# Idle matmuls at the start, a reordered opening, fold copies on ScalarE and Strassen's scheme in half of one second layer

## Chip, core and metric

The kernel runs on one core of one Trainium2 chip. A core has five engines with a queue each: TensorE (PE, matrix products, with its weight loads shown apart as PEld), VectorE (DVE), ScalarE (ACT), GpSimd (POOL) and SyncE (SP, which here issues nearly all DMAs). The metric is device time in microseconds. Five runs of the kernel before gave a median of 847.75 us (846.78 to 854.08).

## The reference

Sparse attention over four batches, eight heads, 768 tokens of 64 channels, followed by a Fourier mixing block with a two-layer network. Everything is float32.

```python
# attention: a band of 2*16-1 neighbours, and 24 block summaries
k_sum = k.reshape(B, H, nb, block, D).max(axis=3)      # block = 32, nb = 24
v_sum = v.reshape(B, H, nb, block, D).mean(axis=3)
scores_l = where(|i - j| < 16, scale * q @ k.T, -1e9)
scores_s = scale * q @ k_sum.T + log(block)
a = softmax(concat(scores_l, scores_s)) ;  out = a @ concat(v, v_sum)
# mixing: x is (4, 768, 512)
mixed = real(fft(fft(x, axis=1), axis=2))
u = x + mixed
un = (u - mean(u)) / sqrt(var(u) + 1e-6)
ch = maximum(un @ w_ch1, 0) @ w_ch2                    # 512 -> 2048 -> 512
return u + ch
```

The two weight matrices arrive as float64 and are turned into float32 on the chip, piece by piece, with bit operations (convert, `words` tiles).

## The kernel before

The program works batch by batch: attention (`gen_attention`), Fourier mixing and normalisation (`gen_fourier`), hidden layer (`gen_hidden`) and output layer (`gen_out`). These are generators; `drive` interleaves their steps, so that attention of the next batch and the Fourier part of the next batch are recorded between the matrix products of the present one. A scheduler then fixes one order for each engine[...]. A `high_priority` of 600 lets attention and Fourier steps move ahead.

**Attention.** A pair of heads (g = 0 to 3, a step of the loop in `gen_attention`) is: load keys and queries, turn them with matmuls (`prepare`, L668 for batch 0, L676 for others, copies on ScalarE L670/L678, block maxima on VectorE L679), scores (L695 and L699 in batch 0, L735 and L751 later), exponentials on ScalarE (L701, L741), a mask product on VectorE (L560), then values (L718, L767). Line L560 is the helper `tt`, so it stands for nearly all VectorE tensor products; groups are told apart by tile names. The values' block sums are made from raw loads (`block_sums`, tiles `vb`, `vbs`): on GpSimd (L563) for most batches, on VectorE for batch 1, whose sums are made early. In batch 0 `sum_values` multiplies them with a selector (L709) and ScalarE copies the result into the values' tile (L710, 1.43 us); this stands ahead of `prepare` for the next pair.

**Fourier part.** The batch's x is folded on VectorE: sums and differences of its halves (tiles `sd`, `zw`, `fg`, all views of `fold`), with three small copies a half (L990, L994, L997). TensorE makes y (L1014 and L1018) from `fold` and a table `fs`, ScalarE copies y (L1020, L1021), TensorE makes mx (L1038, L1040 in batch 0; L963, L965 later), VectorE adds it to x and takes statistics, un is transposed (unt, L1079) into u. In batch 0, `keep_busy` gives TensorE four 128x512 products without use (L952) while the fold runs.

**Hidden layer.** Eight steps j, each by Strassen's seven products on half blocks (L1101, three PSUM tiles X, Y, Z, combined by ScalarE copies L1111, L1116, L1118 and VectorE additions; relus on ScalarE in batch 0 L1108, on VectorE later L1106). Strassen's scheme as used: four sums of left blocks (`_left_sums`, S1 to S4), four of right blocks (`_right_sums`, T1 to T4), seven products, additions.

**Output layer.** `gen_out(b, c)` handles half c of the hidden units. In batches 1 to 3 it uses Strassen's scheme (L1167): left sums of h on VectorE (tiles `s`), right blocks of w2 with their sums in tiles `w2`, 84 products of 128x256. In batch 0 it is a plain product for both c (L1142): 48 products of 128x512, because w2's right sums do not exist yet; they are made in batch 1 (`get_w2`), which loads four blocks, forms three more and writes six back to DRAM for batches 2 and 3.

**Weights.** `gen_weights` follows a hand-written `plan` of pieces, each not before a named stage; `make` converts two halves, adds left sums for w1, and stores the result in DRAM (`dw1`, `dw2`). It runs beside the first batch.

Four PSUM banks serve attention (`abank`), four the rest (`bank`). Tiles with a tag and `bufs=n` share n buffers; a new tile waits for the last reader of the old one.

Of the kernel before, what the change touches and what calls it, by code (L numbers as in the profile page):

```python
# [9 lines left out]
FP = mybir.dt.float32  # L10
# [6 lines left out]
P = 128  # L17
# [469 lines left out]
def _main_program(ctx, tc, q, k, v, moe_w_ch1, moe_w_ch2, out):  # L487


    nc = tc.nc  # L490
    B, H, S, D = q.shape
    DM = H * D
# [91 lines left out]
    def block_sums(b, gg):  # L584

        f = BLOCK // 4
        n = f * D
        if done_weights:
            raw = room(f"vb_{b}_{gg}")
            raw = [raw[0:4 * nb, n * i:n * (i + 1)] for i in range(4)]  # L590
        else:

            raw = [bpool.tile([P, NC, P], FP, tag="s", bufs=5, name=f"vb_{b}_{gg}_{i}").rearrange("p n t -> p (n t)")
                   [0:4 * nb] for i in range(4)]
        for i in range(4):
            fetch(out=raw[i], in_=v[b, 4 * gg:4 * gg + 4].rearrange("h (n f) d -> (h n) (f d)", f=BLOCK)
                  [:, n * i:n * (i + 1)])
        vb = spool.tile([4 * nb, D], FP, tag="vbs", bufs=2, name=f"vbs_{b}_{gg}")

        add = tt if b == 1 else gtt  # L600
        add(raw[0], raw[0], raw[1], ADD)
        add(raw[2], raw[2], raw[3], ADD)
        add(raw[0], raw[0], raw[2], ADD)
        if b == 1:
            nc.vector.tensor_reduce(out=vb, in_=raw[0].rearrange("p (f d) -> p d f", d=D), op=ADD, axis=AX.X)
# [12 lines left out]
        return vw_bufs[g % 2].rearrange("p (e n) d -> p e n d", e=2)  # L618

    def load_values(b, g):  # L620
        if g % 2 and following(b, g, 1):
            block_sums(*divmod((b * NP + g + 1) // 2, NP // 2))
        (load_wide_values if is_wide(b) else load_narrow_values)(b, g)

# [159 lines left out]
    def following(b, g, n):  # L784
        i = b * NP + g + n
        return divmod(i, NP) if i < B * NP else None

    def gen_attention(b):
        x = bpool.tile([P, NST, DM], FP, tag="x", bufs=2, name=f"x_{b}")
        x_of[b] = x  # L790
        for g in range(NP):
            p = (wide_scores if is_wide(b) else scores)(b, g)
            yield
            if is_wide(b):
                sum_values(b, g)
            else:
                sum_scores(b, g, p[1])
            n1, n2 = following(b, g, 1), following(b, g, 2)
            early = (b, g) == (0, NP - 1)
            if early:  # L800
                wide_values(b, g, p, x)
            if n1:
                with tc.issue_after(marks["last av"]) if early else ExitStack():
                    prepare(*n1)

            for n in {(0, 1): (), (0, 2): (2,), (0, 3): (2, 3)}.get((b, g), (3,)):
                n = following(b, g, n)
                if n:
                    load(*n)
            yield  # L810
            if not early:
                if is_wide(b):
                    wide_values(b, g, p, x)
                else:
                    values(b, g, *p, x)
            if n2:
                load_values(*n2)
            if (b, g) == (0, 0):
                load_raw(2)
            yield  # L820


# [47 lines left out]
    def make(f, j):  # L870


        if f == 1:
            w = bpool.tile([P, 7, 2, P], FP, tag="w1", bufs=3, name=f"w1_0_{j}")
            wv, to = w.rearrange("p a k n -> p a (k n)"), dw1[j].rearrange("p a k n -> p a (k n)")
        else:
            w = wv = bpool.tile([P, 7, HD], FP, tag="w2", bufs=NC, name=f"w2_0_{j}")
            to = dw2[j]
        for hh in range(2):
            yield from convert((f, j, hh), wv[:, 2 * hh:2 * hh + 2].rearrange("p a n -> p (a n)"))  # L880
        if f == 1:
            _left_sums(tt, lambda i: wv[:, i])
        else:

            to, wv = to[:, 0:4], wv[:, 0:4]
# [29 lines left out]
    def get_w2(b, j):  # L915
        w = bpool.tile([P, 7, HD], FP, tag="w2", bufs=NC, name=f"w2_{b}_{j}")
        if b == 0:
            return
        wt[2, b, j] = w
        if b == 1:  # L920
            fetch(out=w[:, 0:4], in_=dw2[j][:, 0:4])
            _right_sums(tt, lambda i: w[:, i])
            fetch(out=dw2[j][:, 1:7], in_=w[:, 1:7])
        else:
            fetch(out=w, in_=dw2[j])
# [46 lines left out]
    def gen_fourier(b):  # L972
# [10 lines left out]
        for par in range(2):  # L983
            sd, zw, fg = fold[:, 0], fold[:, 1], fold[:, 2 - 2 * par]
            tt(sd, x[:, 0:HT, :], x[:, HT:NST, :], SUB if par else ADD)
            keep_busy(b, par, sd)
            tt(zw[:, :, 0:HD], sd[:, :, 0:HD], sd[:, :, HD:DM], ADD)
            tt(zw[:, :, HD:DM], sd[:, :, 0:HD], sd[:, :, HD:DM], SUB)
            keep_busy(b, par, zw)
            nc.vector.tensor_copy(out=zq[:, par], in_=zw[:, :, Q])  # L990
            nc.vector.memset(fg[:, :, Q:Q + 1], 0.0)
            tt(fg[:, :, 1:Q], zw[:, :, 1:Q], zw[:, :, HD - 1:Q:-1], ADD)
            tt(fg[:, :, Q + 1:HD], zw[:, :, 1:Q], zw[:, :, HD - 1:Q:-1], SUB)
            nc.vector.tensor_copy(out=fg[:, :, 0:DM:HD], in_=zw[:, :, 0:DM:HD])  # L994
            tt(fg[:, :, HD + 1:HD + Q], zw[:, :, HD + 1:HD + Q], zw[:, :, DM - 1:HD + Q:-1], SUB)
            tt(fg[:, :, HD + Q:DM - 1], zw[:, :, HD + 1:HD + Q], zw[:, :, DM - 1:HD + Q:-1], ADD)
            ins = nc.vector.tensor_copy(out=fg[:, :, DM - 1:DM], in_=zw[:, :, HD + Q:HD + Q + 1])  # L997
            fgs.append(fg)
            yield
        marks["fold", b] = ins.ins  # L1000
# [132 lines left out]
    def gen_out(b, c):  # L1133
        x, h = x_of[b], wt["h", b]
        js = range(NC * c, NC * (c + 1))
        if b == 0:

            for t in range(NST):
                ps = bank([P, DM], f"o_{b}_{c}_{t}")
# [4 lines left out]
                    if n % 2 == 0:  # L1144
                        yield
                tt(x[:, t, :], ps, x[:, t, :], ADD)
                if NC * (c + 1) == NJ:
                    fetch(out=out[b, P * t:P * (t + 1), :], in_=x[:, t, :])
            issued.add(("o", b, c))
            return  # L1150
        for i in range(HT):
# [42 lines left out]

    nc.scalar.dma_start(out=ident, in_=dr["ident"].ap())
    load(0, 0)
    fetch(out=wide, in_=dr["wide"].ap())
    nc.scalar.dma_start(out=count, in_=dr["count"].ap())
    nc.scalar.dma_start(out=sel, in_=dr["sel"].ap())
# [119 lines left out]
```

## Time and profile before

| what | us |
|---|---|
| median of five runs | 847.75 |
| the profiled execution | 847.71 |
| its span on the core | 845.9 |
| TensorE busy / idle in the span | 812.5 / 33.4 |
| output layer of batch 0 on TensorE (L1142, 192 records) | 84.9 |
| longest waits of TensorE: hx for ScalarE's copy of h (5 times) | 6.0 |
| qk for the DMA of keys (2 times) | 5.7 |
| the busy products for the fold (once) | 5.3 |
| value sums for GpSimd's block sums (once) | 3.3 |

How to read it: a float32 product appears as two records in the trace, so 48 products are 96 records. A wait is put down to what came last. Idle time of engines other than TensorE costs nothing by itself.

### The profile page before, as it was taken

The numbers are of one execution on the slowest core, as the hardware profiler recorded it, in microseconds if no ns is written. First come the engines' busy times: TensorE is split into PE (matmuls) and PEld (weight loads), VectorE is DVE, ScalarE is ACT, GpSimd is POOL, SyncE is SP. The second block draws the span as 40 slices with busy tenths as digits, with TensorE's granted clock in tenths as the row PEclk, the third lists the DMA queues.
The fourth block names the chain that finished last, engine by engine and source line by source line (L and its number), as shares of the span: only waits on it lengthen the run. The fifth ranks groups of instructions, "written<-read, shape, count | busy, mean of one in ns | idle before, by whom it ended". The sixth has DMA issues, their size and how long they took to land.

```text
span 845.9 us, 14497 instructions
## 1 busy us (share of the span) xinstructions
PE 812.5 (96%) x6006; PEld 568.5 (67%) x6006; DVE 480.4 (57%) x1115; ACT 230.1 (27%) x473; POOL 38.3 (5%) x44
## 2 busy tenths in 40 slices
PE   5979998999999999999999999999999999999997
PEld 4847755545556555787667875688667885786586
DVE  2487996986976543544357943443337953532352
ACT  3524666552721113122232104120321012101100
POOL 3200012003000200001000000000000000000000
PEclk8989999999999999999999999999999999999999
DMA  9997595979523274454843236403411326205001
GB/s 215 227 281 164 146 243 180 267 247 300 194 79 131 75 273 136 115 112 160 237 107 98 72 131 218 113 24 83 166 60 55 113 63 248 88 1 217 1 27 53
DMA packets 102858, 120.94 MB, mean 143 GB/s; under 512 B 50592, under 2 KB 83584, under 8 KB 102784
## 3 DMA queue, kind: packets, MB, share of 16 engines
q1 hardware_dynamic: 102240, 119.77, 48.7%
q8 instruction: 49, 0.80, 0.4%
q10 hardware_dynamic: 544, 0.17, 0.1%
q14 instruction: 25, 0.20, 0.1%
HBM read 95.80 MB, written 24.12 MB: 142 GB/s over the span
## 4 chain that ended last, share of the span: by engine, by line
PE 80%; DVE 10%; ACT 6%; DMA 2%; issue 1%; ACTq 0%; SPq 0%; DVEq 0%
PE hx L1101 18%; PE ox L1167 13%; PE o L1142 9%; PE hz L1101 9%; PE oz L1167 7%; PE hy L1101 4%; PE y L1014 4%; PE oy L1167 3%; DVE x L560 3%; PE sc L735 2%; PE mx L963 1%; ACT qt L678 1%; ACT kt L678 1%; PE unt L1079 1%; PE sc L695 1%
## 5 line engine op out<-in xcount | busy, mean ns | idle before, releaser
L1101 PE MATMUL hx<-u,w 128*128 128x384 f32 x512 | 186.1, 492 | 8.0 <-ACT h L1111 6.0
L1101 PEld LDWEIGHTS hx<-u,w 128*128 128x128 f32 x512 | 94.6, 190 | 74.5 <-ACT h L1111 9.3
L1101 PE MATMUL hz<-u,w 128*128 128x384 f32 x256 | 93.2, 486 | 0.0
L1142 PE MATMUL o<-w,h 128*128 128x512 f32 x192 | 84.9, 595 | 0.0
L1101 PEld LDWEIGHTS hz<-u,w 128*128 128x128 f32 x256 | 48.7, 190 | 33.9 <-ACT h L1118 0.2
L1167 PE MATMUL ox<-w,s 128*128 128x256 f32 x288 | 69.0, 381 | 0.4 <-DVE x L560 0.3
L1167 PE MATMUL oz<-w,s 128*128 128x256 f32 x288 | 68.7, 379 | 0.0
L1167 PE MATMUL ox<-w,h 128*128 128x256 f32 x288 | 67.0, 380 | 0.0
L1142 PEld LDWEIGHTS o<-w,h 128*128 128x128 f32 x192 | 35.7, 190 | 41.8 <-issue 39.7
L560 DVE TENSOR_TENSOR x<-ox,x 128x256 f32<-128x256 f32 x72 | 30.2, 422 | 55.7 <-PE ox L1167 55.7
L1167 PEld LDWEIGHTS ox<-w,h 128*128 128x128 f32 x288 | 54.5, 190 | 8.3
L1167 PEld LDWEIGHTS ox<-w,s 128*128 128x128 f32 x288 | 54.0, 190 | 8.4 <-DVE x L560 1.2
L1167 PEld LDWEIGHTS oz<-w,s 128*128 128x128 f32 x288 | 54.5, 190 | 7.2
L560 DVE TENSOR_TENSOR h<-hx,h 128x384 f32<-128x384 f32 x32 | 17.8, 556 | 71.2 <-PE hx L1101 71.2
L560 DVE TENSOR_TENSOR h<-hy,h 128x384 f32<-128x384 f32 x32 | 17.8, 556 | 57.2 <-PE hy L1101 54.0
L1111 ACT COPY h<-hx 128x384 f32<-128x384 f32 x32 | 15.3, 477 | 121.6 <-PE hx L1101 109.9
L1101 PE MATMUL hy<-u,w 128*128 128x384 f32 x128 | 46.5, 486 | 0.0
L679 DVE TENSOR_REDUCE km<-kt 128x24 f32<-128x768 f32 x16 | 15.2, 952 | 39.0 <-ACT kt L678 25.1
L1127 ACT ACTIVATE h<-hx 128x384 f32<-128x384 f32 x32 | 15.7, 490 | 79.1 <-PE hx L1101 79.1
L1014 PE MATMUL y<-fs,fold 128*128 128x193 f32 x192 | 37.1, 336 | 0.0
L1014 PEld LDWEIGHTS y<-fs,fold 128*128 128x128 f32 x192 | 31.3, 190 | 7.8 <-issue 6.1
L1101 PEld LDWEIGHTS hy<-u,w 128*128 128x128 f32 x128 | 24.4, 190 | 16.9
(125 smaller groups left out, 1103.6 us busy)
## 6 DMA issues: line engine op xcount, KB each, us to landing
w<-dw SPq DMA_DIRECT2D x40, 896.0 KB, 5.6
words<-in_moe_w_ch_dram SPq DMA_DIRECT2D x32, 512.0 KB, 6.5
vw<-in_v_dram SPq DMA_DIRECT2D x47, 192.0 KB, 5.6
dw<-w SPq DMA_DIRECT2D x8, 896.0 KB, 7.5
kn<-in_k_dram SPq DMA_DIRECT2D x16, 384.0 KB, 4.8
qn<-in_q_dram SPq DMA_DIRECT2D x16, 384.0 KB, 5.5
vb<-in_v_dram SPq DMA_DIRECT2D x32, 192.0 KB, 5.2
out_dram<-x SPq DMA_DIRECT2D x24, 256.0 KB, 2.5
```

Source lines behind the costliest of these rows:

```text
L560: nc.vector.tensor_tensor(out=out, in0=in0, in1=in1, op=op)
L678: nc.scalar.copy(out=dst[D * e:D * (e + 1), s:S:2], in_=ps[D * s:D * (s + 1)])
L679: nc.vector.tensor_reduce(out=km[:, 0:nb], in_=kt[:, W:W + S].rearrange("p (n f) -> p n f", f=BLOCK), op=ALU.max, axis=AX.X)
L695: nc.tensor.matmul(ps[e][0:WK, n - n0, :], kt[rows, QB * n:QB * n + WK], qt[rows, QB * n:QB * (n + 1)], start=True, stop=True)
L735: nc.tensor.matmul(ps[h][r:r + 64, i, :], kt[rows, o:o + 64], qt[rows, o:o + BLOCK], start=True, stop=True)
L963: nc.tensor.matmul(out, y[:, g], table, start=True, stop=last, skip_group_check=True)
L1014: nc.tensor.matmul(y, fgs[par][:, st, P * g:P * (g + 1)], fs[par][:, g % 2, st, :], start=(st == 0), stop=(st == HT - 1))
L1101: nc.tensor.matmul(ps, w[:, a, kk, :], u[:, r, kk, :], start=start and kk == 0, stop=stop and kk == 1, skip_group_check=True)
L1111: nc.scalar.copy(out=c11, in_=X)
L1127: nc.scalar.activation(out=c21, in_=X, func=AF.Relu)
L1142: nc.tensor.matmul(ps, h[:, n, hf, P * t:P * (t + 1)], wt[2, b, j][:, 2 * hf:2 * hf + 2, :], start=(n, hf) == (0, 0), stop=(n, hf) == (NC ...
L1167: nc.tensor.matmul(ps, left[a][:, n, :], wt[2, b, j][:, r, :], start=start and n == 0, stop=stop and n == NC - 1, skip_group_check=True)
```

## The change

Six edits:

- Two products of a zeroed tile are put at the very start on TensorE; the tile is zeroed by GpSimd.
- In the first head pair of batch 0, `sum_values` comes after `prepare` of the next pair, and the first weight loads come ahead of the value loads for g = 2.
- Block sums for batch 1: the first half goes to GpSimd; the second stays on VectorE and moves from the attention of batch 1 to the end of the Fourier part of batch 0.
- Left sums of the first w1 piece wait until the fold of batch 0 is done.
- The three small copies of the fold go from VectorE to ScalarE.
- `gen_out(0, 1)` uses Strassen's scheme. So `make` forms the right sums of w2 for j = 4 to 7 and stores all seven blocks, and batch 1 loads these seven instead of forming and writing them.

```diff
@@ block_sums
-        add = tt if b == 1 else gtt
+        add = tt if (b, gg) == (1, 1) else gtt
...
-        if b == 1:
+        if (b, gg) == (1, 1):
             nc.vector.tensor_reduce(out=vb, in_=raw[0].rearrange("p (f d) -> p d f", d=D), op=ADD, axis=AX.X)
@@ load_values
-        if g % 2 and following(b, g, 1):
+        if g % 2 and following(b, g, 1) and (b, g) != (1, 1):
             block_sums(*divmod((b * NP + g + 1) // 2, NP // 2))
@@ gen_attention
-            if is_wide(b):
+            if not is_wide(b):
+                sum_scores(b, g, p[1])
+            elif g:
                 sum_values(b, g)
-            else:
-                sum_scores(b, g, p[1])
...
                 with tc.issue_after(marks["last av"]) if early else ExitStack():
                     prepare(*n1)
+            if (b, g) == (0, 0):
+                sum_values(b, g)
...
+            if (b, g) == (0, 0):
+                load_raw(2)
             if n2:
                 load_values(*n2)
-            if (b, g) == (0, 0):
-                load_raw(2)
@@ make
-        if f == 1:
+        if (f, j) == (1, 0):
+            while ("fold", 0) not in issued:
+                yield
+            with tc.issue_after(marks["fold", 0]):
+                _left_sums(tt, lambda i: wv[:, i])
+        elif f == 1:
             _left_sums(tt, lambda i: wv[:, i])
-        else:
+        elif j < NC:
             to, wv = to[:, 0:4], wv[:, 0:4]
+        else:
+            _right_sums(tt, lambda i: wv[:, i])
@@ get_w2
-        if b == 1:
+        if b == 1 and j < NC:
             fetch(out=w[:, 0:4], in_=dw2[j][:, 0:4])
             _right_sums(tt, lambda i: w[:, i])
             fetch(out=dw2[j][:, 1:7], in_=w[:, 1:7])
@@ gen_fourier
-            nc.vector.tensor_copy(out=zq[:, par], in_=zw[:, :, Q])
+            nc.scalar.copy(out=zq[:, par], in_=zw[:, :, Q])
...
-            nc.vector.tensor_copy(out=fg[:, :, 0:DM:HD], in_=zw[:, :, 0:DM:HD])
+            nc.scalar.copy(out=fg[:, :, 0:DM:HD], in_=zw[:, :, 0:DM:HD])
...
-            tt(fg[:, :, HD + Q:DM - 1], zw[:, :, HD + 1:HD + Q], zw[:, :, DM - 1:HD + Q:-1], ADD)
-            ins = nc.vector.tensor_copy(out=fg[:, :, DM - 1:DM], in_=zw[:, :, HD + Q:HD + Q + 1])
+            nc.scalar.copy(out=fg[:, :, DM - 1:DM], in_=zw[:, :, HD + Q:HD + Q + 1])
+            ins = nc.vector.tensor_tensor(out=fg[:, :, HD + Q:DM - 1], in0=zw[:, :, HD + 1:HD + Q],
+                                          in1=zw[:, :, DM - 1:HD + Q:-1], op=ADD)
@@ gen_out
-        if b == 0:
+        if (b, c) == (0, 0):
...
-                if NC * (c + 1) == NJ:
-                    fetch(out=out[b, P * t:P * (t + 1), :], in_=x[:, t, :])
@@ the start of the program
     load(0, 0)
+    zeros = bpool.tile([P, 7, 2, S2], FP, tag="u", name="zeros").rearrange("p a k n -> p (a k n)")[:, 0:640]
+    nc.gpsimd.memset(zeros, 0.0)
+    ps = bank([P, 512], "warm")
+    for i in range(2):
+        nc.tensor.matmul(ps, zeros[:, 512:640], zeros[:, 0:512], start=True, stop=True)
@@ the end of the program's opening
     drive((gen_fourier(0), 4, 600), (first(weights, 66), 12, 0), (first(attn, 5), 1, 0))
+    block_sums(1, 1)
```

More of the change, by code (lines that the diff above doesn't have):

```diff
@@ L880, in make @@
             yield from convert((f, j, hh), wv[:, 2 * hh:2 * hh + 2].rearrange("p a n -> p (a n)"))
-        if f == 1:
+        if (f, j) == (1, 0):
[4 more added lines that the diff above has]
+        elif f == 1:
             _left_sums(tt, lambda i: wv[:, i])
+        elif j < NC:
+            to, wv = to[:, 0:4], wv[:, 0:4]
         else:
-            to, wv = to[:, 0:4], wv[:, 0:4]
+            _right_sums(tt, lambda i: wv[:, i])
         yield
```

## The prediction, made blind

> **What bounds the kernel now.** I read the page first, for the shares.
>
> ```profile
> PE 812.5 (96%) x6006; PEld 568.5 (67%) x6006; DVE 480.4 (57%) x1115; ACT 230.1 (27%) x473; POOL 38.3 (5%) x44
> ```
>
> TensorE is busy 812.5 of 845.9 us, so time comes off in two ways only: less matmul work where TensorE never waits, or less of its 33 us of idle time. The second view is busy time by stretch (columns: length, PE, PEld, DVE, ACT and POOL busy with counts, granted clock, DMA share, GB/s).
>
> ```profile
> 0.00:20.00 20.00, 10.76 (x122) 8.89 (x124) 5.79 (x15) 6.28 (x10) 6.64 (x12) 0.90 1.03 216
> 40.00:60.00 20.00, 13.93 (x195) 10.42 (x192) 16.90 (x35) 7.92 (x14) 0.27 (x2) 0.92 1.14 283
> 280.00:300.00 20.00, 20.00 (x57) 9.49 (x56) 8.45 (x10) 2.11 (x3) 5.63 (x5) 1.00 0.25 81
> ```
>
> The idle time lies in the first 60 us (9.2 and 6.1 us); in the stretch where the first batch's second layer ends there is none. The third view is the chain of waits of the first 70 us (start, length, what).
>
> ```profile
> 9.65 8.87 DMA kn<-in_k_dram
> 18.52 0.14 issue
> 18.66 4.76 PE qk L668 x48
> 23.42 1.44 PE av L718 x44
> ...
> 53.16 0.10 DVE rec L723
> 53.27 0.94 DVE vbs L605
> 54.20 0.47 DVE x L560
> 54.67 0.60 DVE words L862
> 55.27 0.11 DVE rec L723
> 55.37 0.57 DVE words L864
> 55.94 0.47 DVE x L560
> 56.41 0.60 DVE w L560
> 57.01 1.68 DVE fold L560
> 58.68 0.04 issue
> 58.73 5.24 PE busy L952 x6
> 63.97 0.98 PE y L1014 x6
> ```
>
> Two places count. Until 18.52 the path is the landing of the second head pair's keys, behind a DMA share of 1.03. From 53.16 to 57.01 it is VectorE, where block sums (vbs) and weight conversion (words, w) stand between the last attention output and the fold. The last view, the timeline of TensorE and ScalarE:
>
> ```profile
> 17.17 0.64 PE L709 MATMUL vs<-vbs,sel 96*32 96x64 f32 x4 [3.33 <-POOL vbs L563]
> 17.84 1.43 ACT L710 COPY vw<-vs 32x1536 f32<-32x1536 f32 x1 [3.10 <-PE vs L709]
> 282.36 21.62 PE L1142 MATMUL o<-w,h 128*128 128x512 f32 x50
> ```
>
> The value sums and their copy run today inside the wait for the keys, where they cost nothing.
>
> [...] the granted clock is 0.50 from 16 to 22 us and from 58 to 62 us, and the fall at 56.8 us comes 3.3 us after the last attention matmul (53.42). It also fell at 15.8 us with work until 13.84[...]. [...] 128x512 records are 0.429 us apart (21.46 us for 50), 128x256 ones 0.216 us (1.73 us for 8): halving costs 0.7%. [...]
>
> **The change, part by part.** The sum is made against the profiled execution, 847.71 us (span 845.9 and 1.8 around it), which is 0.04 below the median of the five runs.
>
> *Idle matmuls.* A memset on GpSimd (nearest rows: 0.10 us for 128x1, 1.27 us for a 96x512 add, so 0.1 to 1.6 us) and two 128x512 matmuls. At the cold rate of the busy row, 5.24 us for 6 records, their 4 records take 3.5 us and end near 4.8 us, when the first keys land (4.82). The first transposes (2.83 us for 24 records, 1.53 us for 24 at 28.99) may shrink, some 2 us with the queries. All of it ends in front of the keys that land at 18.52: SyncE issues them at 9.65[...]. Value 0; range -0.6 to 0.
>
> *Next keys ahead of the first value sums.* In the built order TensorE now runs scores, the 48 key and query records, the value sum, the attention values. Keys still land at 18.52, so turning ends at 23.4. Then the sum's matmul (about 0.4) and ScalarE's copy of 1.43 us behind its last query copy (ends 23.88): the values start near 25.5 instead of 23.24, +2.2 us. Until 53.4 TensorE has almost no slack (19.84 of 20 us busy from 20 to 40), so the shift is carried. Bounds +1.4 (part overlaps) and -0.6 (keys land before the sums). The weight loads now issued ahead of the values of g=2 cost nothing: those values land near 37 us today (last issue about 29, 8 us to landing) and are used at 41.86. The words arrive sooner and let conversion fill VectorE (8.02 of 20 us busy from 20 to 40).
>
> *Block sums off VectorE, left sums after the fold.* On the chain, vbs 0.94, words 0.60 and 0.57 and w 0.60 leave: -2.7 us. In the built order only two reciprocals and two x products stand before the fold. GpSimd does these sums in about 7 us (six adds, 10.56 to 17.11), needed only at 92 us. The sums of (1,1), 2.9 us, fall into VectorE's work near 135 us instead of among the statistics. With +2.2 the fold starts near 56.5 instead of 57.01.
>
> *Fold and its copies.* Three copies a half, 0.16 us each on VectorE (0.07 in a row), go to ScalarE. [...] ScalarE idles 13.11 us before its first y copy, so they hide[...]. The fold loses also the w sums that stand inside it (0.41, 0.41, 0.87): it ends near 67.3 instead of 69.8. The matmuls that keep TensorE busy, 5.24 us, block y until 63.97. In the new version TensorE idles from 55.6 to 58.2, 2.6 us, not 5.31. If the clock stays up, three busy matmuls take 2.6 us (0.86 each, as the fourth at 64.95) and y starts near 61: -2.6 beyond the shift; if it falls, -0.3. The drop at 15.8 forbids certainty: I take -1.5. Behind y TensorE is dense (19.24 of 20 us), so the gain is carried.
>
> *First hidden half.* hx waits 6.0 us in all for ScalarE's h copy; the waits at 133.73 (1.39) and 147.68 (1.12) have conversion pieces ahead of that copy which the new order puts behind it. Value -0.8, bounds -2.5 and +1.
>
> *Strassen in gen_out(0, 1).* Before: 48 matmuls of 128x512, 96 records at 0.429 = 41.2 us. After: 3 row pairs x 7 products x 4 = 84 matmuls, 168 records at 0.216 = 36.3 us: -4.9 us. VectorE gets 12 left sums (0.62 each in a row, 7.4 us) and 21 additions at 0.42 (8.9 us) for six at 0.60. Batches 1 and 2 run this very stage: from the first o matmul to the next hidden layer 440.94 to 500.78 is 59.84 us and 634.97 to 694.75 is 59.78, against 240.40 to 303.82 = 63.42 us in batch 0. I take the measured difference, -3.6, not -4.9; bounds -2.5 and -4.9.
>
> *Its right sums.* Sixteen 128x256 operations at 0.34 in a row (four in 1.35 us at 397.39), 5.4 us, enter VectorE before 240 us, where conversion ran without a gap from 213.24 to 234.04 and then idled 3.31 us. They end near 239.4, so the addition for hx of j=7 (238.09) comes about 1.3 us late. Four PSUM banks cover most: +0.5; bounds 0 and +5.4. The stores of the seven blocks (0.9 MB instead of 0.5, four times) delay the tables behind them on SyncE's queue: fm is issued near 240 and lands 8 us later, needed at 258. DMA share there is 0.27.
>
> *Batch 1.* For j of 4 to 7 the right sums (5.4 us of VectorE) and the store back go; the loads grow by 0.4 MB each. TensorE waited there 0.25 us (402.38): -0.2.
>
> Sum: +2.2 -2.7 -1.5 -0.8 -3.6 +0.5 -0.2 = -6.1, so 841.6 us.
>
> **The rivals.** (1) *Only Strassen counts* (chance 0.27): the clock falls before the fold, the values come 2.2 us late and ScalarE's waits stay. Then +2.2 -2.7 -0.3 -3.6 +0.5 = -3.9: 843.8 us. [...] Against: two fewer conversions ahead of h copies. (2) *VectorE becomes the bound before the fold of batch 1* (0.07), the slower side: between 205 and 240 us its queue already sets the pace, and right sums (5.4) and the two left sums put into the fold (1.2) fall on the path in full, the table load following them. With the stage gaining nothing net (-3.6 given back by late s sums) and the opening at -0.5 net, 847.7 + 6.6 - 0.5 = 853.8 us. It decides from the point where less than 2 of VectorE's roughly 11.8 idle us of 200 to 240 can be used. Against it: half of that idle time is waiting for hx, which sums placed ahead can fill. (3) *More is gained* (0.12): full 4.9 us of Strassen, the clock stays up, ScalarE waits shrink by 2: 2.2 -2.7 -2.6 -2.0 -4.9 = -10: 837.7 us. That the change doesn't do what it says I exclude: the built order shows the 84 matmuls.
>
> **How the numbers follow.** Forecast 0.54, rivals 0.27, 0.07, 0.12. Its own spread is 839 to 844. The range of 80% runs from 837.5 to 846.5, leaving out the slower case and the outer edges. About 0.5% (843.5 and 852.0) can be told from no change. Faster: 0.46 of the forecast's 0.54, 0.12 of (3) and some of (1): 0.61. Slower: most of (2): 0.06. The rest, 0.33, is within.
>
> **What would show it.** Matmuls of gen_out(0, 1) as 168 records of 128x256, and the stage at 60 us. The first value copy near 24 us and values at 25.5. Fold at 56.5 with nothing between it and the x products; y at 61 with clock 1.00, or 63.6 with 0.50. Wrong if keys land before 15 us, if hx waits for VectorE between 205 and 240, or if the stage keeps 63 us.

## The result, and the profile after

The changed kernel is slower: a median of 852.35 us (42 runs) against 848.2 us for the kernel before (79 runs on the same chip), a ratio of 1.005 with a 95% interval of 1.0038 to 1.0061. Ratios are worked out from the fast runs alone, medians from all; left out as slow, over 1.5% above the fastest of the same kernel, are two runs of the changed kernel and three of e1_late_sums. The profiled execution took 850.28 us (span 848.2), 2.6 us more than the one before.

The record also has TensorE's mean granted clock for every run. In the changed kernel it lies between 0.972 and 0.990 and goes with the time (correlation -0.96 over 44 runs): 19 of the 44 are under 0.985, with a median of 856.4 us, and the other 25 have a median of 850.4. Of the runs of the kernel before that were taken beside the experiments, 8 of 152 are under 0.985. So a good part of the loss is a clock that is low more often, but runs that keep it up are still some 2 us slower than the kernel before. The profiled execution, at 0.989, is one of these.

Busy time by engine, from the page of the changed kernel:

```profile
PE 814.4 (96%) x6082; PEld 584.9 (69%) x6082; DVE 488.5 (58%) x1114; ACT 234.0 (28%) x497; POOL 45.0 (5%) x51
```

TensorE has 1.9 us more to do, not less: Strassen took matrix work away (its 84 products run in 59.3 us of stage instead of 63.4), but the idle products (3.78 us for their four records) and stretches at half clock (17.1 us of them, 13.7 in the kernel before) put more back. Busy time by stretch, columns as in the prediction:

```profile
0.00:20.00 20.00, 13.61 (x133) 9.36 (x135) 4.55 (x15) 5.33 (x10) 7.19 (x13) 0.91 1.02 217
20.00:40.00 20.00, 18.48 (x291) 14.59 (x287) 8.55 (x17) 9.91 (x18) 6.27 (x7) 0.92 1.08 229
40.00:60.00 20.00, 16.82 (x210) 12.96 (x208) 12.57 (x24) 8.41 (x14) 4.77 (x7) 0.91 1.03 277
200.00:210.00 10.00, 6.92 (x116) 4.21 (x115) 9.03 (x19) 2.48 (x4) 2.56 (x4) 0.71 0.75 147
```

The last stretch in the kernel before:

```profile
200.00:210.00 10.00, 9.55 (x117) 5.93 (x99) 4.87 (x11) 3.19 (x7) 1.24 (x1) 1.00 0.96 236
```

TensorE now idles between 20 and 40 us, where it had almost no slack before, and between 200 and 210 us, where the clock also falls to a mean of 0.71. The chain of waits of the first 70 us:

```profile
8.96 8.29 DMA kn<-in_k_dram
17.39 5.39 PE qk L668 x48
22.78 0.58 PE vs L709 x4
23.38 1.44 ACT vw L710
24.86 1.73 PE av L718 x48
...
40.28 3.16 DVE p L560 x2
43.45 0.47 DVE x L560
44.06 3.22 PE qk L668 x26
...
60.24 0.57 DVE x L560
60.83 1.77 DVE fold L560
62.64 2.99 PE busy L961 x6
65.63 0.98 PE y L1024 x6
```

The first value copy (L710) is on the chain now, as forecast. Nothing stands between the last x product and the fold, as forecast too; but the fold starts at 60.83 us, not at 56.5: attention of batch 0 ended at 59.96 us instead of 53.42. From its first values on it took 35.10 us instead of 30.18: 2.2 us more of idle time (TensorE waits 2.3 us for rec at 44 us, behind p on VectorE), 1.4 us lost to the clock, which is at half from 43.7 to 47.1 us, and 1.3 us of longer busy time. The second loss, from the timeline near 200 us (start, length, engine, line; in brackets the idle time before and what ended it):

```profile
193.18 7.16 POOL L563 TENSOR_TENSOR vb<-vb,vb 96x512 f32<-96x512 f32 x3 [51.79 <-DMA vb<-in_v_dram]
...
197.46 1.76 DVE L864 SCALAR_TENSOR_TENSOR words<-words 128x512 int32<-128x512 int32 x1
199.13 1.75 DVE L560 TENSOR_TENSOR w<-words 128x512 f32<-128x512 f32 x1
...
203.37 1.09 DVE L560 TENSOR_TENSOR w<-w 128x256 f32<-128x256 f32 x3
204.39 0.28 DVE L560 TENSOR_TENSOR vs<-vs,half 128x128 f32<-128x128 f32 x1
...
204.72 1.67 PE L772 MATMUL av<-vs,p 64*128 64x130 f32 x12 [3.08 <-DVE vs L560]
206.32 3.78 PE L1152 MATMUL o<-w,h 128*128 128x512 f32 x4
```

TensorE waits 3.08 us for vs, which stands in VectorE's queue behind conversions and right sums (w<-w), two of the conversions taking 1.75 us instead of the usual 0.68 while GpSimd adds. Then the clock falls to 0.50, from 204.2 to 211.0 us: four o records take 3.78 us. In the kernel before, a conversion beside GpSimd's adds, which run from 191.92 us on, takes 1.75 us too, but vs comes in time and the clock stays at 1.00:

```profile
193.67 1.75 DVE L864 SCALAR_TENSOR_TENSOR words<-words 128x512 f32<-128x512 uint32 x1
...
201.32 0.94 PE L772 MATMUL av<-vs,p 64*128 64x130 f32 x12 [0.45 <-DVE vs L560]
202.19 1.98 PE L1142 MATMUL o<-w,h 128*128 128x512 f32 x4
```

The differences at the milestones (start of the stage; after minus before, us):

| milestone | before | after | difference |
|---|---|---|---|
| first attention values | 23.24 | 24.86 | +1.6 |
| end of batch 0's attention | 53.42 | 59.96 | +6.5 |
| first y | 63.81 | 65.47 | +1.7 |
| first hidden half | 104.40 | 105.58 | +1.2 |
| second hidden half | 204.01 | 209.90 | +5.9 |
| second output half of batch 0 | 240.40 | 246.84 | +6.4 |
| hidden layer of batch 1 | 303.82 | 306.10 | +2.3 |
| output layer of batch 1 | 349.38 | 353.25 | +3.9 |
| end of TensorE's work | 839.90 | 842.21 | +2.3 |

So Strassen's stage gives 4.2 us and 1.6 of it goes in the next row; the losses are the attention of batch 0, of whose 6.5 us all but 1.7 are won back by the first y, and the stretch from the first to the second hidden half, where 4.7 us go; later batches give 1.6 back.

### The profile page after: what moved, and what is told of

Same layout as the page of the kernel before. It is cut to its first block, busy times and chain, and to the rows that moved or that the text cites. A ratio compares the mean times of both kernels' runs of the same rounds, so it can differ in the third digit from the quotient of the medians.

```text
span 848.2 us, 14682 instructions
## 1 busy us (share of the span) xinstructions
PE 814.4 (96%) x6082; PEld 584.9 (69%) x6082; DVE 488.5 (58%) x1114; ACT 234.0 (28%) x497; POOL 45.0 (5%) x51
## 4 chain that ended last, share of the span: by engine, by line
PE 82%; DVE 9%; ACT 5%; DMA 2%; issue 1%; ACTq 0%; SPq 0%
PE hx L1111 18%; PE ox L1175 16%; PE hz L1111 9%; PE oz L1175 8%; PE hy L1111 4%; PE y L1024 4%; PE oy L1175 4%; PE o L1152 3%; PE sc L735 2%; PE mx L972 2%; ACT qt L678 2%; DVE x L560 2%; DVE w L560 2%; ACT kt L678 2%; PE qk L668 1%; PE sc L695 1%
## 5 line engine op out<-in xcount | busy, mean ns | idle before, releaser
L1175 PE MATMUL ox<-w,s 128*128 128x256 f32 x336 | 80.7, 381 | 0.2
L1175 PE MATMUL oz<-w,s 128*128 128x256 f32 x336 | 80.5, 379 | 0.0
L1175 PE MATMUL ox<-w,h 128*128 128x256 f32 x336 | 78.0, 380 | 0.0
L560 DVE TENSOR_TENSOR x<-ox,x 128x256 f32<-128x256 f32 x84 | 35.3, 422 | 61.2 <-PE ox L1175 61.1
L1175 PEld LDWEIGHTS ox<-w,h 128*128 128x128 f32 x336 | 63.5, 190 | 9.6
L1175 PEld LDWEIGHTS ox<-w,s 128*128 128x128 f32 x336 | 62.9, 190 | 9.3 <-DVE x L560 1.0
L1175 PEld LDWEIGHTS oz<-w,s 128*128 128x128 f32 x336 | 63.6, 190 | 8.3
L1152 PE MATMUL o<-w,h 128*128 128x512 f32 x96 | 44.5, 617 | 0.3 <-DVE w L560 0.3
L1175 PE MATMUL oy<-w,h 128*128 128x256 f32 x168 | 39.7, 379 | 0.0
L679 DVE TENSOR_REDUCE km<-kt 128x24 f32<-128x768 f32 x16 | 15.2, 952 | 37.5 <-ACT kt L678 27.9
```

Source lines behind the costliest of these rows:

```text
L560: nc.vector.tensor_tensor(out=out, in0=in0, in1=in1, op=op)
L679: nc.vector.tensor_reduce(out=km[:, 0:nb], in_=kt[:, W:W + S].rearrange("p (n f) -> p n f", f=BLOCK), op=ALU.max, axis=AX.X)
L1152: nc.tensor.matmul(ps, h[:, n, hf, P * t:P * (t + 1)], wt[2, b, j][:, 2 * hf:2 * hf + 2, :], start=(n, hf) == (0, 0), stop=(n, hf) == (NC ...
L1175: nc.tensor.matmul(ps, left[a][:, n, :], wt[2, b, j][:, r, :], start=start and n == 0, stop=stop and n == NC - 1, skip_group_check=True)
```

## The experiments

Twelve kernels ran, in three sets. Ratios are to the kernel before on the same chip, with their 95% intervals; the profiled column is the one profiled execution (before: 847.71), and the last counts the runs whose mean granted clock was under 0.985 (before: 8 of 152). The first and third set ran on one chip, the second on another, each beside its own runs of the kernel before.

| kernel | median us | ratio | interval | profiled us | low clock |
|---|---|---|---|---|---|
| changed | 852.35 | 1.0050 | 1.0038 to 1.0061 | 850.28 | 19 of 44 |
| e1_late_sums | 845.55 | 0.9951 | 0.9933 to 0.9970 | 847.67 | 5 of 22 |
| e2_first_sums_vector | 850.03 | 1.0023 | 1.0001 to 1.0045 | 847.01 | 4 of 14 |
| e3_strassen_alone | 847.12 | 0.9983 | 0.9971 to 0.9995 | 846.47 | 0 of 22 |
| e4_opening_alone | 851.25 | 1.0043 | 1.0023 to 1.0064 | 849.85 | 6 of 22 |
| f1_fold | 845.39 | 0.9968 | 0.9951 to 0.9986 | 845.74 | 5 of 22 |
| f2_idle | 844.63 | 0.9968 | 0.9950 to 0.9987 | 843.40 | 1 of 14 |
| f3_blocks | 848.44 | 0.9992 | 0.9972 to 1.0012 | 850.33 | 7 of 14 |
| f4_order | 854.97 | 1.0070 | 1.0042 to 1.0098 | 850.72 | 8 of 14 |
| g1_keys | 846.74 | 0.9986 | 0.9967 to 1.0005 | 846.66 | 1 of 14 |
| g2_words | 853.11 | 1.0044 | 1.0026 to 1.0063 | 853.00 | 17 of 21 |
| g3_late | 841.15 | 0.9917 | 0.9898 to 0.9937 | 840.38 | 0 of 6 |
| g4_late_both | 840.98 | 0.9915 | 0.9898 to 0.9933 | 840.32 | 0 of 6 |

### First set: parts taken out of the changed kernel

Theory 1 was that GpSimd's block sums hold VectorE up; theory 2 that the right sums in VectorE's queue do, whatever GpSimd does.

**e1_late_sums**: block sums of batch 2's first half later.

```diff
-        if g % 2 and following(b, g, 1) and (b, g) != (1, 1):
+        if g % 2 and following(b, g, 1) and (b, g) not in ((1, 1), (1, 3)):
...
     for b in range(B):
+        if b == 1:
+            block_sums(2, 0)
```

> The changed kernel, but GpSimd adds the value blocks of batch 2's first half only when batch 1's hidden stage starts (near 305 us), no longer from 193 to 200 us. Theory 1 [...]: the conversions at 197 to 201 us fall back from 1.2 to 1.8 us each to about 0.7 us, the last vs product comes near 202 us, TensorE's 3.1 us wait for it falls under 0.7 us, the clock stays at 1.00 from 204 to 211 us, and the kernel is 4 to 6 us faster than the changed one (843 to 845 in the measure of its profile's 850.3). Theory 2 (the right sums of w2 number 4 stand ahead of vs in VectorE's queue, whatever GpSimd does): the wait stays above 1.5 us, the clock still falls, and the gain is under 2 us.

The expectation named the wrong sums. Those at 193 us belong to batch 2's second half; the first half's ran at 133 to 141 us. The edit took the latter away from there and put them at 196 us, and the second half's at 292. So GpSimd still adds near 200 us, and conversions there still take 1.22 and 1.75 us. All the same TensorE waits only 1.2 us for vs (3.1 in the changed kernel), the clock stays at 1.00 there, and the ratio went from 1.0050 to 0.9951, the largest gain of the set (0.8% by the medians). The wait shrank, then, but not because GpSimd was idle beside it, as theory 1 would have it. Nor do the sums at 133 us show as a wait of TensorE in this kernel: its waits for h come to 3.0 us in both traces. What they cost is taken up with g3_late. The profiled execution isn't typical: it lost 8.3 us of clock in the attention of batch 0, which ended at 62.81 us.

**e2_first_sums_vector**: sums of batch 1's first half back on VectorE.

```diff
-        add = tt if (b, gg) == (1, 1) else gtt
+        add = tt if b == 1 else gtt
```

> The changed kernel, but the value blocks of batch 1's first half are added by VectorE again, in their place of the kernel before. Theory 1: the attention-0 operation on p that took 1.58 us twice near 40 us takes about 0.5 us again, the 2.25 us wait for rec at 44 us falls under 0.7 us, and the last attention matmul of batch 0 ends 2 to 3 us before 59.96. VectorE has about 7 us more work between 30 and 60 us, so at most 1 us of it shows elsewhere: 1 to 3 us faster than the changed kernel in all. Rival (the order of the value loads and sums makes rec late, not GpSimd): the wait at 44 us stays above 1.5 us and the kernel is no faster, or slower by up to 2 us for VectorE's extra work.

As theory 1 has it: no wait for rec at 44 us, attention of batch 0 over at 56.77 us (3.2 earlier), 0.27% faster, though the intervals overlap. But 56.77 is still 3.3 us later than before, with the clock at 1.00 from 22 to 58 us. Something else in the opening costs more.

**e3_strassen_alone** and **e4_opening_alone**: the two halves of the change. e3 is the kernel before with this; e4 is the changed kernel without it.

```diff
@@ make
+        elif j < NC:
             to, wv = to[:, 0:4], wv[:, 0:4]
+        else:
+            _right_sums(tt, lambda i: wv[:, i])
@@ get_w2
-        if b == 1:
+        if b == 1 and j < NC:
@@ gen_out
-        if b == 0:
+        if (b, c) == (0, 0):
```

> The kernel before with the Strassen stage of batch 0's second half alone, its right sums included; idle matmuls, opening order, GpSimd's sums and the fold stay as before. If the loss near 205 us belongs to the moved block sums (theory 1): the stage takes 59.0 to 60.0 us instead of 63.4, the second hidden half starts within 1.5 us of 204.0, and the kernel is 3 to 4.5 us faster than before. If the right sums in VectorE's queue are the cause (theory 2): the second hidden half starts 3 us or more late and the kernel is within 1 us of before.

> The changed kernel with the second layer of batch 0's second half done plainly again (no right sums there, the stage of 63.4 us). Theory 1 (block sums): VectorE's conversions near 200 us are still stretched above 1.1 us, vs is late by at least 1 us at 204 us, and the kernel is 4 to 9 us slower than before. Theory 2 (right sums): no stall at 204 us, the second hidden half starts within 1.5 us of 205.2, and the kernel is 1 to 2.5 us slower than before, which is what the opening lost at the first hidden matmul (105.58 against 104.40).

In e3 the stage took 59.44 us, as expected, and the second hidden half started at 203.64, so theory 2 alone is out: with the right sums in place the wait for vs was 0.8 us (0.4 before). The gain, though, was 0.17%, 1.4 us, not 3 to 4.5. The missing part is visible in the next stage. VectorE and TensorE in e3, as batch 1's hidden layer starts:

```profile
306.64 1.56 DVE L560 TENSOR_TENSOR w<-w 128x256 f32<-128x256 f32 x4 [1.66 <-DMA w<-dw]
308.12 0.55 DVE L560 TENSOR_TENSOR h<-hx,h 128x384 f32<-128x384 f32 x1
...
308.72 1.56 PE L1102 MATMUL hx<-u,w 128*128 128x384 f32 x4 [1.34 <-DVE h L560]
```

The blocks of w2 for batch 1 are loaded when they were before (SyncE issues them at 298.4 and 300.6 us, the first at 298.9 in the kernel before, behind the output stores), but the hidden layer now starts 4.3 us sooner. Their right sums wait for the DMA at the head of VectorE's queue, and the addition to h behind them is late. From that start to the output layer of batch 1 e3 needs 47.19 us, the kernel before 45.56: 1.6 of the 4.0 us are lost. TensorE still ended 2.9 us earlier than before in the profiled execution, but the end of that execution lay 7.7 us behind its last product (6.0 in the kernel before). The interval allows a gain of 0.4 to 2.5 us, so 2.9 doesn't quite fit; what the rest is, one profile can't say.

e4 holds the whole loss: 1.0043. Its wait for vs was 1.5 us with the clock at 1.00; the changed kernel's 3.1 us thus contains about 1.6 us that come with the right sums. Both theories have a part in that wait. Beside this opening Strassen gains nothing measurable (1.0050 with it, 1.0043 without): in the profiled execution its 4.2 us are used up by 1.6 at vs, 3.0 of clock after that wait, and 1.6 at batch 1's first stage, against 2.1 us of clock that e4's execution lost near 100 us.

### Second set: the opening's parts, added one at a time

f1_fold is the base: e3 and the fold part of the change, nothing else of it.

```diff
@@ make (on e3)
-        if f == 1:
+        if (f, j) == (1, 0):
+            while ("fold", 0) not in issued:
+                yield
+            with tc.issue_after(marks["fold", 0]):
+                _left_sums(tt, lambda i: wv[:, i])
+        elif f == 1:
@@ gen_fourier
-            nc.vector.tensor_copy(out=zq[:, par], in_=zw[:, :, Q])
+            nc.scalar.copy(out=zq[:, par], in_=zw[:, :, Q])
...
-            nc.vector.tensor_copy(out=fg[:, :, 0:DM:HD], in_=zw[:, :, 0:DM:HD])
+            nc.scalar.copy(out=fg[:, :, 0:DM:HD], in_=zw[:, :, 0:DM:HD])
...
-            ins = nc.vector.tensor_copy(out=fg[:, :, DM - 1:DM], in_=zw[:, :, HD + Q:HD + Q + 1])
+            nc.scalar.copy(out=fg[:, :, DM - 1:DM], in_=zw[:, :, HD + Q:HD + Q + 1])
```

> The kernel before with the Strassen stage and, of the other parts, only the fold's three copies on ScalarE and the first left sums put after the fold. Idle matmuls, the order of keys and value sums, the loads' order and the block sums are those of before. Theory A (the opening's loss comes from the order of keys and value sums and from the block sums, not from here): about 3 us faster than before, that is the 1.2 us of Strassen alone, 1.35 us in the folds of the later batches (in the four kernels run so far the time from batch 1's last stage to the end was 397.6 us with the copies on ScalarE and 399.0 without), and 0.5 to 1 us at the first fold; the runs spread as narrowly as those of before. Rival (ScalarE's copies delay the first fold): within 1 us of Strassen alone.

0.9968, 2.7 us faster than before, and 0.15% under e3 with overlapping intervals. From the second output half of batch 1 to the end it took 397.78 us against 399.01 in e3, and so it is in all traces: 397.6 to 397.8 us in the twelve with the copies on ScalarE, 399.0 in the two without. The copies pay in the later folds (1.2 us in all). At the first fold they paid nothing: from the end of attention to y both took 10.59 us.

**f2_idle**, **f3_blocks** and **f4_order** each add one more part to f1_fold: the idle products; the two lines on block sums and where batch 1's second half is added; the order in `gen_attention`.

```diff
@@ f2_idle: start of the program
+    nc.gpsimd.memset(zeros, 0.0)
...
+        nc.tensor.matmul(ps, zeros[:, 512:640], zeros[:, 0:512], start=True, stop=True)
@@ f3_blocks: block_sums, load_values, end of the opening
+        add = tt if (b, gg) == (1, 1) else gtt
...
+        if g % 2 and following(b, g, 1) and (b, g) != (1, 1):
...
+    block_sums(1, 1)
@@ f4_order: gen_attention
+            if (b, g) == (0, 0):
+                sum_values(b, g)
...
+            if (b, g) == (0, 0):
+                load_raw(2)
             if n2:
                 load_values(*n2)
```

> The kernel f1_fold with the idle matmuls on zeros added at the start. Theory A (they end before the first keys land and nothing waits for them): the same as f1_fold within 1 us, though the first queries are turned about 1 us earlier. Rival (they keep the clock up through the second keys' wait): 1 to 2 us faster. Second rival (they change which clock falls come later): the attention of batch 0 ends later than in f1_fold by more than 1 us.

> The kernel f1_fold with the block sums moved as in the change: those of batch 1's first half by GpSimd near 40 us, those of its second half after the first transform. Theory 1 (GpSimd's adds and VectorE hold each other up): p near 40 us takes 1 us or more an operation, TensorE waits 1 to 2.5 us for rec there, after which its clock falls in some executions; against that vbs (0.94 us) leaves the stretch ahead of the fold. 0 to 3 us slower than f1_fold, with a wider spread. Rival (GpSimd is free, as I forecast): 1 to 2 us faster than f1_fold.

> The kernel f1_fold with the next keys turned ahead of the first value sums and the words loaded ahead of the later values, as in the change. Theory A (the order is the main loss of the opening): the first attention values start 1 to 1.5 us later than in f1_fold, TensorE waits 1.5 us for the value copy, and a further 1 to 2 us are lost until the attention of batch 0 ends; 2 to 4 us slower than f1_fold. Rival (the value copy only moves a wait, keys landing earlier pay for it): within 1 us of f1_fold.

The idle products change nothing that can be measured (0.9968 both). In f2_idle's profiled execution the clock falls inside the attention of batch 0, which ends at 54.19 us instead of 52.64, and yet y starts at 63.23 us in both: f1_fold's clock is low too, from 56.5 to 63.4 us, where TensorE waits for the fold and runs the busy products. Block sums on GpSimd start the fold 2.3 us earlier (53.85 against 56.14) and y with it (60.94 against 63.23), and lose it again: a 3.7 us wait for vs ahead of the second hidden half, then half clock from 201.7 to 208.5 us. In total 0.24% slower than f1_fold, with overlapping intervals: no clear effect on the time, though 7 of 14 runs have a low clock. The expected wait for rec at 42 us didn't come, so with the old order GpSimd's sums at 41 to 50 us cost the attention only 0.3 us. The order of `gen_attention` is the loss: 1.0070, 1.0% slower than f1_fold, the intervals far apart.

### Third set: which half of the order, and a better version

**g1_keys** and **g2_words** are f1_fold with one half of f4_order each.

```diff
@@ g1_keys
-            if is_wide(b):
+            if not is_wide(b):
+                sum_scores(b, g, p[1])
+            elif g:
                 sum_values(b, g)
-            else:
-                sum_scores(b, g, p[1])
...
+            if (b, g) == (0, 0):
+                sum_values(b, g)
@@ g2_words
+            if (b, g) == (0, 0):
+                load_raw(2)
             if n2:
                 load_values(*n2)
-            if (b, g) == (0, 0):
-                load_raw(2)
```

> The kernel f1_fold with one edit of the change: the next keys are turned ahead of the first value sums; the words are still loaded after the later values. Both edits together (f4_order) ended the attention of batch 0 at 56.8 us instead of 52.6 and cost about 1% of the whole time. Theory K (the keys' edit is the loss): the first attention values start near 24.2 us instead of 22.5, TensorE waits 1.5 us for the value copy, and the kernel is 1.5 to 3 us slower than f1_fold from this alone. Theory W (the words' edit is the loss): the values start 1.5 us later, the attention ends less than 2 us later, and the kernel is less than 2 us slower.

> The kernel f1_fold with the other edit alone: the words of the weights are loaded ahead of the later values, and keys and value sums stand as before. Theory W: conversion pieces move ahead of attention work on VectorE and ScalarE and the later values land late, so that TensorE waits near 55 us for a value copy or for the values, the attention of batch 0 ends 2 us or more later than in f1_fold (52.6 us), the hidden layer of batch 0 waits 2 us more, and the kernel is 4 to 8 us slower than f1_fold. Theory K: within 1.5 us of f1_fold.

Loading the words ahead of the values is the loss: 1.0044 against 0.9968, 0.76% or 6.4 us. The keys' order costs 0.18%, with overlapping intervals. As expected, g2_words is 4 to 8 us slower than f1_fold and its attention of batch 0 ends later; but the attention isn't late by waiting: TensorE is idle for 0.6 us only between its first values and the end of attention. The order of its own matmuls is different. f1_fold's timeline of TensorE, third pair's values and fourth pair's scores:

```profile
41.19 0.98 PE L718 MATMUL av<-vw,p 128*64 128x65 f32 x26
42.09 1.23 PE L695 MATMUL sc<-qt,kt 64*96 64x64 f32 x12
43.25 0.83 PE L699 MATMUL sc<-qt,km 64*32 64x384 f32 x2
44.01 0.86 PE L718 MATMUL av<-vw,p 128*64 128x65 f32 x21
```

The same in g2_words:

```profile
41.26 0.55 PE L695 MATMUL sc<-qt,kt 64*96 64x64 f32 x4
41.73 0.33 PE L718 MATMUL av<-vw,p 128*64 128x65 f32 x2
41.99 0.38 PE L695 MATMUL sc<-qt,kt 64*96 64x64 f32 x2
42.30 0.33 PE L718 MATMUL av<-vw,p 128*64 128x65 f32 x2
42.56 0.38 PE L695 MATMUL sc<-qt,kt 64*96 64x64 f32 x2
...
44.26 0.83 PE L699 MATMUL sc<-qt,km 64*32 64x384 f32 x2
45.02 0.91 PE L718 MATMUL av<-vw,p 128*64 128x65 f32 x10
```

The two kinds alternate in twos; one turn takes 0.57 us. In blocks, two sc records take 0.19 us (1.16 us for 12) and an av record 0.035 (0.90 for 26). In f4_order the stretch with these values, 12 score records and their two block records took 4.96 us (42.86 to 47.82), in f1_fold 3.52 (41.19 to 44.71), both at full clock. The changed kernel alternates in twos and fours at 47.7 to 50.3 us, and so do all kernels run here that load the words first; g1_keys, which doesn't, has one such turn. In g2_words the clock goes soon after it; busy time by stretch in g2_words:

```profile
44.00:48.00 4.00, 4.00 (x28) 3.07 (x28) 1.16 (x2) 1.01 (x2) 0.00 (x0) 0.62 1.05 360
48.00:52.00 4.00, 4.00 (x18) 2.32 (x18) 1.27 (x4) 0.86 (x2) 0.14 (x1) 0.50 1.01 403
```

It is at 0.50 from 45.0 to 58.6 us. Attention of batch 0 ends at 59.02 us instead of 52.64; of the 7.3 us by which the stretch from the first values on is longer, 6.7 are busy time lost to the clock (busy time times one less the clock, added over 2 us stretches). The profiled executions of f1_fold and g2_words (845.74 and 853.00) lie at their medians.

That is half of the account. By the first y (66.71 us against 63.23) 2.9 of the 6.4 us are won back, as with f2_idle. Another 3.8 us go between the first and the second hidden half, which lie 105.02 us apart instead of 101.22, while the clock takes the same 1.6 us in both. There TensorE waits longer for VectorE (what waited for what, us in total, times, longest; between 102 and 212 us). In f1_fold:

```profile
PE av L772 <- DVE vs L560: 0.7, 1, 0.7
```

In g2_words:

```profile
PE av L772 <- DVE vs L560: 2.5, 1, 2.5
PE o L1150 <- DVE w L560: 1.0, 2, 0.7
```

In f4_order the loss is almost all here: 0.8 us at the first y, 3.8 more between the two hidden halves (105.01 us). Why VectorE falls behind there when the words come first was not followed further.

The clock of all runs fits two parts. In g2_words 17 of 21 runs have a low clock, in f1_fold 5 of 22. Among the others, four and 17 runs, the medians are 848.0 and 844.5 us, so some 3.6 us are lost with the clock up.

That the alternation makes the clock fall is not shown, and it can't be the only cause: f2_idle and g3_late lost 2.5 and 3.0 us of clock in the attention of batch 0 without it, f4_order and e4_opening_alone had it and kept the clock there, and in the changed kernel the clock fell at 43.7 us, before the alternation at 47.7.

**g3_late** and **g4_late_both** are f2_idle with the edit of e1 (and, in g4, with `block_sums(1, 1)` after the first transform).

```diff
-        if g % 2 and following(b, g, 1):
+        if g % 2 and following(b, g, 1) and (b, g) != (1, 3):
...
+        if b == 1:
+            block_sums(2, 0)
```

> The kernel f2_idle with the value blocks of batch 2's first half added by GpSimd later: in the changed kernel this edit moved them from 133 to 196 us and those of batch 2's second half from 193 to 292 us, and made it about 8 us faster. Theory 1 (GpSimd's adds hold VectorE up where VectorE has no slack): the same or 1 to 2 us faster than f2_idle, since in f2_idle TensorE waits 1.6 us for h from VectorE while GpSimd adds between 123 and 130 us. Rival (the gain existed only because the changed order had filled VectorE): within 0.7 us of f2_idle.

> The kernel g3_late with the value blocks of batch 1's second half added after the first transform, as in the change, but those of batch 1's first half still by VectorE in their old place. Expected: vbs (0.94 us) and what comes with it leave the stretch ahead of the fold, so the first y comes 1 to 2.5 us earlier than in g3_late (f3_blocks had it at 60.9 us instead of 63.2). If the 2.9 us of VectorE near 135 us hide, this is the fastest of all, near 841 to 843 us; if they come on the path to the second hidden half, as the 3.7 us wait for vs in f3_blocks says, it is no faster than g3_late.

g3_late has 0.9917 against 0.9968 for f2_idle, intervals apart. What it removes shows in f2_idle, near the first hidden layer of batch 0:

```profile
123.28 4.12 POOL L563 TENSOR_TENSOR vb<-vb,vb 96x512 f32<-96x512 f32 x3 [68.88 <-DMA vb<-in_v_dram]
124.78 1.50 DVE L858 TENSOR_SCALAR words<-words 128x512 int32<-128x512 int32 x1
126.20 0.54 DVE L560 TENSOR_TENSOR h<-hx,h 128x384 f32<-128x384 f32 x1
...
126.80 1.56 PE L1109 MATMUL hx<-u,w 128*128 128x384 f32 x4 [1.59 <-DVE h L560]
```

and in g3_late, where GpSimd is idle then:

```profile
124.04 0.42 DVE L858 TENSOR_SCALAR words<-words 128x512 int32<-128x512 int32 x1
124.37 0.55 DVE L560 TENSOR_TENSOR h<-hx,h 128x384 f32<-128x384 f32 x1
...
124.98 1.56 PE L1109 MATMUL hx<-u,w 128*128 128x384 f32 x4 [0.52 <-DVE h L560]
```

One 0.42 us operation takes 1.50 us, and TensorE pays 1.07 us for it. From the first to the second hidden half f2_idle needs 100.34 us and g3_late 97.69; there is no wait for vs left. e1_late_sums, which has the whole opening of the change and these sums late as well, is 0.34% slower than g3_late (0.5% by the medians), with intervals that just overlap. So with these sums away all the other moves of the opening together cost less than the words alone did in f1_fold (0.76%): the prices depend on what else is in the kernel. g4_late_both is the same within the interval. Its expectation was wrong about what it moves: vbs ahead of the fold belongs to batch 1's first half, which stays there, so y isn't earlier (10.59 us after the end of attention). With six runs each, g3_late and g4_late_both are 0.83% and 0.85% faster than the kernel before.

## Why the prediction was wrong

The forecast was 841.6 us, faster; the kernel takes 852.35, outside the range. Its own steps, in order:

- *Idle matmuls*, nothing: right (f2_idle). The first queries are turned earlier and the time is lost ahead of the second keys.
- *Next keys ahead of the first value sums*, +2.2: the mechanism is right (the copy is exposed, TensorE waits 1.5 us), the size +1.1 in g1_keys and +1.6 in the changed kernel at the first values.
- **The step that failed** stands in that paragraph: "The weight loads now issued ahead of the values of g=2 cost nothing: those values land near 37 us today". The landing was the only thing priced, and the term was put at nothing. Alone, on f1_fold, this edit costs 0.76%, 6.4 us. The runs showed three things in its place: TensorE's own matmuls stand in another order, values and scores alternating (1.4 us in f4_order at full clock); the clock is low in 17 of 21 runs instead of 5 of 22; and TensorE waits longer for VectorE ahead of the second hidden half, where 3.8 us go. The built order shows the alternation; the argument looked at the order at the start and at the fold, not at the pairs between. The edit was not taken out of the changed kernel itself, so its price there is carried over from f1_fold.
- *Block sums off VectorE*, -2.7: right at the fold (-2.3 in f3_blocks). "GpSimd does these sums in about 7 us, needed only at 92 us" was the error: GpSimd's time was free but VectorE's wasn't. In the changed kernel p took 3.16 us for two operations at 40 us (1.03 before) beside GpSimd's adds, and taking these adds off GpSimd again (e2) ended the attention 3.2 us earlier, 1.4 of them clock.
- *Fold and its copies*, -1.5: from the fold's start to y 4.8 us instead of 6.96, so -2.2, within the bounds, but by luck: that the clock would stay up was an estimate. It did in this execution, and in f1_fold, which has the same copies and where it fell, the fold to y took what it took in e3 (7.08 us both). Each copy took 0.19 to 0.20 us on ScalarE. Missed: the later folds gain 1.2 us by the copies.
- *First hidden half*, -0.8: TensorE's idle time there fell from 4.3 to 3.1 us, -1.2.
- *Strassen*, -3.6: -4.2 in the stage. Missed: what starts sooner must find its loads there; 1.6 us go at once into a wait for the DMA of batch 1's w2.
- *Right sums*, +0.5: no loss between 205 and 240 us, the place that was looked at (36.39 us before, 36.4 without the clock). They cost about 1.6 us at 204 us (0.4 in e3, without the new opening), a place just ahead of it, in the queue ahead of vs.
- *Batch 1*, -0.2: 91.35 us instead of 91.56.

None of the three signs that were to show it wrong came: keys land at 17.3 us, hx waits for VectorE nowhere between 205 and 240 us, the stage takes 59.3 us. The time was lost where no sign stood. Of the rivals, the slow one gave 853.8 us, near what was measured, but that is luck, since the mechanism is another: VectorE does become the bound, yet ahead of the second hidden half and beside GpSimd, not from 205 to 240 us. The sum also had no term for a fall of the clock outside the start and the fold. In the profiled execution of the changed kernel the falls at 43.7 and 204.2 us cost 1.4 and 3.0 us, and over all its runs the clock is low in 19 of 44.

The parts don't add up. One by one they come to 0.9% slower (Strassen -0.17, the fold -0.15, idle products 0, block sums +0.24, the order +1.02), the whole change to 0.5%: they act on each other.

What stays open: what makes the clock fall, why VectorE falls behind ahead of the second hidden half when the words come first, and why the scheduler alternates then. Not tried were the changed kernel without the words' edit, and moving the second half's sums away from 195 us.

## What to carry to other kernels

An edit to the order of loads can also change the order of everything that a scheduler places by their times: compare the order of the busiest engine's own instructions over the whole stretch, not only the wait that was meant. Work moved to GpSimd was not free here: beside its adds two operations of VectorE on p took 3.16 us instead of 1.03. Moving it in time (g3_late) was worth more (0.5%) than moving it between engines. A stage made shorter starts the next one sooner, and its loads have to move as well: in e3, where they didn't, 1.6 of the 4.0 us were lost again. And one profile is one execution: read it beside the clock of all runs (low in 17 of 21 against 5 of 22 here).

## What the runs showed of the hardware

Operations of VectorE took longer beside GpSimd's adds. In f3_blocks

```profile
41.40 1.52 POOL L563 TENSOR_TENSOR vb<-vb,vb 96x512 f32<-96x512 f32 x1 [14.13 <-DMA vb<-in_v_dram]
41.71 1.76 DVE L862 SCALAR_TENSOR_TENSOR words<-words 128x512 int32<-128x512 int32 x1
```

the conversion, 0.68 us otherwise, begins inside the add and ends 0.55 us after it. The operation that took 1.50 us instead of 0.42 in f2_idle has one tensor input, the two products on p that took 3.16 us in the changed kernel (1.03 before) have two. Not every operation was stretched: in the changed kernel the block maximum at 20.66 us (L679) took 0.95 us beside an add, and 0.95 at 7.67 us, where GpSimd was idle. The adds differed as well: three of them took 3.94 us there, with only this one operation on VectorE, 4.44 (1.27 and 3.17) in the kernel before near 193 us, and 7.16 in the changed kernel near 195 us, both with VectorE busy.

The clock fell while TensorE's records left no gap: in g2_words TensorE is busy 4.00 of 4.00 us in the stretches at 40 and 44 us, and the clock goes to 0.50 at 45. What made it fall is not in the trace. In the traces of the two kernels, of f3_blocks, of f4_order and of the four kernels of the third set, each stretch at half clock before the last product lasted 3.4, 6.8 or 13.7 us. Executions of one kernel differ with the clock: those of the changed kernel go from 847.3 us at a mean clock of 0.990 to 861.7 us at 0.972.
